# Chunk 0's state output as seven block products behind the last input projection, with two more rotations by transferred additions

## The chip, the cores and the metric

The kernel runs on one core of one Trainium2 chip. The metric is device time in microseconds (us), the median of several executions. Beside it stands one execution taken by the hardware profiler, with its span from the first to the last instruction and its trace. The engines are TensorE (PE, matmuls), VectorE (DVE), ScalarE (ACT), GpSimd (POOL, here mostly issuing DMAs that add) and SyncE (SP, issuing plain DMAs). A name such as L762 is a line of the kernel file.

## What is computed

The input `x` has 2048 rows of 512. It is normalised by row to `xn`, and three things are summed: `x` itself, a diagonal state-space layer on `xn`, and a gated feed-forward layer on `xn`.

```
xn   = layernorm(x)
Bu   = xn @ B_bar.T                      # complex, 512 states
h[t] = Lam_bar * h[t-1] + Bu[t]          # over all 2048 rows
y    = 2 * Re(h @ C.T) + xn * Dskip
ffn  = (silu(xn @ w_gate) * (xn @ w_up)) @ w_down     # 1376 hidden columns
out  = x + y + ffn
```

Matmuls take bf16 and sum in f32; the output is bf16.

## The kernel before

**Chunks.** The rows are cut into four chunks of 512 rows, and a chunk into four row tiles of 128. The transposed normalised input stands in `xnT`, one chunk after another. TensorE's order of stages, after a start-up for chunk 0, is: input projection (`bproj_chunk`, L974, 32 matmuls) and gate/up projection (`gateup_chunk`, L985, 84 matmuls) of chunks 0 and 1, projection of chunk 2, feed-forward output of chunk 0 (`out_ffn`, L743), two half tiles that chunks share (`up_halves`, L531), state output of chunk 0 (`out_ssm`, L753), gate/up of chunk 2, projection of chunk 3, feed-forward output of chunk 1, the rows of the last short hidden tile (`out_rows`, L591), state output of chunk 1 as seven products (`out_ssm_seven`, L644), gate/up of chunk 3, and the last pair of chunks (`out_pair`, L713).

**State layer.** A recurrence with complex factors is made real by a rotation: `u` is turned by a table of cosines and sines (`c16`, `s16`), scanned with a real decay (L459, eight scans per chunk), and turned back into `wt`. `rotation` (L384) does a turn with six VectorE instructions. `rotation_dma` (L413) does it with four and leaves two additions to GpSimd's DMAs, which add while they write; it needs a negated sine table `neg_s16`, which stands in the first chunk's columns of `xnT` once these have been used. Before, chunk 2's back rotation and chunk 3's forward rotation go this way.

**State output.** `out_ssm` multiplies `wt` (real and imaginary parts, 4 row blocks each) by `CF`, 32 matmuls of 512 columns for a chunk. `out_ssm_seven` does the same block matrix product with seven products of half size instead of eight (56 matmuls of 256 columns), with sums of blocks made beforehand: of the states by `state_sums` (L628), of the weights by `weight_sums` (L612). A sum is a copy by ScalarE, negated or not (`signed_copy`, L603), and a DMA that adds (`added`, L609). Afterwards VectorE puts the products together in f32 scratch that lies in a used gate/up buffer. Chunks 1 and 2 go this way before. Chunk 0's output sums stay in four of the eight PSUM banks from `out_ffn` until `out_rows` has added its part; then ScalarE copies them out (`out_leave`, L774) and a DMA adds them to the output, which already holds `x`.

**Order.** The order on each engine is that of the program text. VectorE's share of the state layer, of the normalisation and of the coefficients (`c_ops`, L354) is kept in a list, `backlog`, each item with a planned cost. `pump(us)` (L800) is called after each group of matmuls with its planned time and emits items while the time owed covers half the next one's cost; `need(tag)` emits all that is left up to the last item of a tag. `products` holds the gate times up multiplications, emitted by `multiply`. `spend` (L964) emits items of the list `sums`, the copies and additions of the block sums, some after each tile.

**Buffers that matter here.** All eight PSUM banks come from one pool. `gu_last` has two buffers, for even and odd chunks; L553 writes one and L527 (in `product_last`) reads it. `up_halves` emits L527 of chunks 0 and 1.

Of the kernel before, what the change touches and what calls it, by code (L numbers as in the profile page):

```python
# [10 lines left out]
F32 = mybir.dt.float32  # L11
BF16 = mybir.dt.bfloat16
ALU = mybir.AluOpType
# [10 lines left out]
def kernel(  # L24
# [52 lines left out]
    def flat(ap3):  # L77
        return ap3.rearrange("p q j -> p (q j)")
# [327 lines left out]

    neg_s16 = xnT[:, :, 0:CW]

    def negate_table():
        for q in range(NQ):  # L410
            nc.scalar.activation(out=neg_s16[:, q], in_=s16[:, q], func=ACT.Copy, scale=-1.0)

    def rotation_dma(src, dst, back):  # L413

        box = {}
        sines = (s16[:], neg_s16) if back else (neg_s16, s16[:])

        def side(i):
            t = box[i] = ssm.tile([128, NQ, CW], BF16, name="pm", bufs=3)
            V.tensor_tensor(out=t[:], in0=src()[:, i], in1=sines[i], op=ALU.mult)  # L420

        def main(i):
            V.tensor_tensor(out=dst()[:, i], in0=src()[:, i], in1=c16[:], op=ALU.mult)

        def join(i):
            nc.gpsimd.dma_start(out=dst()[:, i], in_=box[1 - i][:], accum_op=ALU.add)
# [59 lines left out]
    u_pair = {}  # L486
    products = []

# [6 lines left out]
    def gu_tile(c):  # L495
        if c not in gu_tiles:
            gu_tiles[c] = gut.tile([128, FT - 1, CW], BF16, name="guT")
        return gu_tiles[c]

    def u_tile(c, fi):  # L500
        if (c, fi // 2) not in u_pair:
            u_pair[c, fi // 2] = up_p.tile([128, 2, CW], BF16, name="u2")
        return u_pair[c, fi // 2]

    def product(c, fi):
        g, u = gu_tile(c)[:, fi - 1:fi + 1, :], u_tile(c, fi)[:]
        products.append(lambda: V.tensor_tensor(out=g, in0=g, in1=u, op=ALU.mult))  # L507
# [91 lines left out]
    TQ = [CT[:, i // 2, :, (i % 2) * HD:(i % 2 + 1) * HD] for i in range(4)]  # L599
    neg_b22 = BT[:, 1, :, 0:HD]  # L600
    parts = {NT - 1: part_end, NT - 2: jidx}

    def signed_copy(out, in_, sign):  # L603

        for lo in range(0, NQ, 2):
            yield lambda lo=lo: nc.scalar.activation(out=out[:, lo:lo + 2], in_=in_[:, lo:lo + 2], func=ACT.Copy,  # L606
                                                     scale=sign)

    def added(out, in_):  # L609
        yield lambda: nc.gpsimd.dma_start(out=out, in_=in_, accum_op=ALU.add)  # L610

    def weight_sums():  # L612

        (b11, b12), (b21, b22) = BQ
        t1, t2, t3, t4 = TQ
        for out, in_, sign, to, add in ((t3, b12, -1.0, t3, b22), (t1, b11, -1.0, t1, b12), (t2, b11, 1.0, t2, t3),
                                        (t4, b22, -1.0, t4, t1)):
            yield from signed_copy(out, in_, sign)
            yield from added(to, add)
        yield from added(t4, b21)  # L620

# [4 lines left out]
    s_tiles = {}  # L626

    def state_sums(c):  # L628

        (a11, a12), (a21, a22) = state_quarters(c)  # L630
        if c == 1:
            s1, s2, s3 = (ssm.tile([128, NQ, HW], BF16, name="cm", bufs=3) for _ in range(3))
            s4 = jidx[:].bitcast(BF16).rearrange("p (q j) -> p q j", q=NQ)
        else:
            s1, s2, s3, s4 = ((wg_g, wu_g)[i // 2][2][:, :, (i % 2) * HD:(i % 2 + 1) * HD] for i in range(4))
        s_tiles[c] = (s1, s2, s3, s4)
        for out, in_, sign, to, add in ((s1, a21, 1.0, s1, a22), (s3, a21, -1.0, s3, a11), (s2, a11, -1.0, s2, s1),
                                        (s4, a12, -1.0, s4, s2)):
            yield from signed_copy(out, in_, sign)
            yield from added(to, add)  # L640
        if c == 1:
            yield from signed_copy(neg_b22, BQ[1][1], -1.0)

    def out_ssm_seven(c):  # L644
# [4 lines left out]
        first = c * TPC  # L649
        space = flat(gu_tiles[c][:]).bitcast(F32).rearrange("p (s j) -> p s j", j=HD)  # L650
        high, low = (space[:, a:a + 4].rearrange("p (i h) j -> p i h j", h=2) for a in (2, 6))
        u2, five = high[:, :, 1], space[:, 0:2]

# [14 lines left out]
        def add(out, in0, in1):  # L668
            V.tensor_tensor(out=out, in0=in0, in1=in1, op=ALU.add)
            owed[0] -= 0.69  # L670
# [21 lines left out]
        x = taken(s1, t1)  # L692
        nc.scalar.copy(out=five, in_=x[:])
        if c == 1:
# [3 lines left out]
        seven = taken(s3, t3)  # L698
        add(low[:, :, 1], u2, five)
        skipped(0, low)  # L700
        product(a22, t4, at(1, 0), False, True)
        add(high[:, :, 0], seven[:], u2)
        add(high[:, :, 1], high[:, :, 0], five)
        skipped(1, high)
        product(s4, neg_b22, at(0, 1), False, True)
        if c == 1:
# [6 lines left out]
    def out_pair(c):  # L713

        multiply(0)
        for n in [*parts, *range(c * TPC, NT - len(parts))]:
            o_tiles[n] = [bank()]
        for op in state_sums(c):
            op()
# [10 lines left out]
        need(f"ssm{c}")  # L730
        need("skip")
        need(f"ssm{c + 1}")
        for n, part in parts.items():
# [229 lines left out]

    def spend(n, late=False):  # L964

        while n and sums:
            if sums[0] is None:
                if not late or any(item[3] == "ssm1" for item in backlog):
                    return
                sums[0:1] = state_sums(1)  # L970
            sums.pop(0)()
            n -= 1

    def bproj_chunk(c):  # L974
        need(f"ln{c}")
        for part in range(2):
            for q in range(NQ):
                bproj_tile(c, part, q)
                pump(BP)
                multiply(0 if q else 1)  # L980
                spend(1, c == NCH - 1)
                if c == NCH - 1 and part == 1 and q == 0:
                    load_rows()

    def gateup_chunk(c):  # L985
        for fi in [FT - 1, *range(FT - 1)]:
            gateup_tile(c, fi)
            pump(GU)
            multiply(1)
            spend(2)  # L990

    def out_chunk(c):

        multiply(0)
        for n in range(c * TPC, (c + 1) * TPC):
            out_ffn(n)
            pump(FT * 0.2163)
            if c == 1:
                spend(4, True)
# [5 lines left out]
        if c == 1:  # L1005
            for step in range(3):
                for k in range(2):
                    out_rows(k, step)
            for n in range(TPC):
                out_leave(n, o_tiles[n][0], opool.tile([128, D], BF16, name="res"))  # L1010
        need(f"ssm{c}")
        need("cf")
        if c == 1:
            spend(99, True)
            return out_ssm_seven(c)
        for n in range(c * TPC, (c + 1) * TPC):
            out_ssm(n)
            pump(2 * NQ * 0.2163)

# [16 lines left out]
    for part in range(2):  # L1036
        for q in range(NQ):
# [10 lines left out]
           ["ln2"] * len(norm2) + ["ln3"] * (len(stats3) + len(norm3)))  # L1048
    queue("cf", c_ops())
    load_late()  # L1050
# [7 lines left out]

    bproj_chunk(1)
    fwd1, back1, _ = ssm_ops(1)  # L1060
    queue("ssm1", fwd1 + back1)
    gateup_chunk(1)
# [4 lines left out]
    out_chunk(0)  # L1067
    sums += [*weight_sums(), None]
# [41 lines left out]
```

## Time and profile before

| what | value |
|---|---|
| median of 3 runs | 176.64 us (176.63 to 177.19) |
| the profiled execution, its own time | 177.04 us |
| its span | 175.2 us |
| granted TensorE clock, mean | 1.000 |
| DMA traffic | 21.36 MB, mean 122 GB/s |

A busy share is the time in which an engine had an instruction under way, as a share of the span. In a timeline each line gives the start, the length, the engine, the line of the kernel and the tile names (out<-in); a bracket tells how long the engine was idle before and what ended that. The chain lists, in order of time, the work that led without a gap to the last instruction. In the rows by stretch of time each engine has its busy time and, in brackets, its number of instructions; the last three columns are the granted clock, the busy share of the 16 DMA engines and what they moved in GB/s. A share a little above 1 comes from how packets are booked.

### The profile page before, as it was taken

To read this page: it belongs to the slowest core of one execution; us is meant where nothing else is said; L and a number is where in the kernel's file an instruction comes from. 1 tells how busy PE (TensorE), PEld (TensorE's weight loads), DVE (VectorE), ACT (ScalarE), POOL (GpSimd) and SP (SyncE) were. 2 spreads that over 40 slices of the span, in tenths; PEclk is the share of its full clock that TensorE was granted. 3 is DMA by queue.
4 is the path that set the end of the run, shared out by engine and by line. 5 is a ranking of instruction groups with operands and counts; after the bars stand their busy time and mean duration, and the time that the engine had idled before them with its cause. 6 is when DMAs were issued, how large, how long until landed. Compare 5 with 4: busy or idle time off the path is not lost.

```text
span 175.2 us, 2790 instructions
## 1 busy us (share of the span) xinstructions
PE 171.7 (98%) x1002; PEld 88.4 (50%) x1002; DVE 161.1 (92%) x248; ACT 107.6 (61%) x204; POOL 45.9 (26%) x49
## 2 busy tenths in 40 slices
PE   8999999999999999999999999999999999999993
PEld 2977544444444444444444444468444444447743
DVE  4779998999999997999999999999999999995884
ACT  5487898868598669772998699052486691001100
POOL 6050120000400130000352224136544841211440
PEclk9999999999999999999999999999999999999999
DMA  6998496995332013700399449339898999955034
GB/s 170 294 170 226 91 250 117 362 230 121 77 76 30 0 30 75 254 4 11 43 105 120 60 51 194 61 60 136 139 156 153 157 175 192 122 60 60 0 105 139
DMA packets 38974, 21.36 MB, mean 122 GB/s; under 512 B 22016, under 2 KB 38144, under 8 KB 38944
## 3 DMA queue, kind: packets, MB, share of 16 engines
q0 software_dynamic: 9552, 8.26, 34.0%
q1 hardware_dynamic: 28016, 12.30, 31.1%
q10 hardware_dynamic: 1392, 0.62, 1.3%
q8 instruction: 8, 0.13, 0.3%
q14 instruction: 6, 0.05, 0.1%
HBM read 8.33 MB, written 4.19 MB: 71 GB/s over the span
## 4 chain that ended last, share of the span: by engine, by line
PE 98%; DVE 0%; issue 0%
PE ps L492 35%; PE ps L380 16%; PE ps L724 10%; PE ps L750 10%; PE ps L762 8%; PE ps L657 7%; PE ps L851 2%; PE ps L828 2%; PE ps L550 2%; PE ps L932 2%; PE ps L595 2%; PE ps L539 1%; PE ps L245 1%; DVE res L767 0%; PE ps L275 0%
## 5 line engine op out<-in xcount | busy, mean ns | idle before, releaser
L492 PE MATMUL ps<-xnT,wg 128*128 128x512 bf16 (+1 forms) x148 | 36.6, 373 | 0.0
L492 PE MATMUL ps<-xnT,wu 128*128 128x512 bf16 (+1 forms) x148 | 36.6, 373 | 0.0
L459 DVE TENSOR_TENSOR_SCAN g<-r_t,car,u 128x512 bf16<-128x512 f32 x24 | 28.7, 1264 | 0.0
L380 PE MATMUL ps<-xnT,BT 128*128 128x512 bf16 x128 | 28.3, 379 | 0.0
L511 ACT ACTIVATE guT<-ps 128x512 bf16<-128x512 f32 (+1 forms) x40 | 24.0, 599 | 5.4 <-PE ps L492 3.4
L512 ACT CAST u<-ps 128x512 bf16<-128x512 f32 (+1 forms) x40 | 23.3, 583 | 4.7 <-PE ps L492 4.5
L492 PEld LDWEIGHTS <-wu 128*128 128x128 bf16 x148 | 14.5, 98 | 16.6
L492 PEld LDWEIGHTS <-wg 128*128 128x128 bf16 x148 | 14.4, 98 | 16.5
L382 ACT CAST u<-ps 128x512 bf16<-128x512 f32 x32 | 18.2, 586 | 4.0 <-PE ps L380 3.9
L380 PEld LDWEIGHTS <-BT 128*128 128x128 bf16 x128 | 12.5, 98 | 14.9
L750 PE MATMUL ps<-wd_sb,guT 128*128 128x512 bf16 x80 | 17.6, 379 | 0.0
L724 PE MATMUL ps<-wd_sb,guT 128*128 128x512 bf16 x80 | 17.4, 379 | 0.0
L214 POOL TENSOR_TENSOR rstd<-ve,neg_half 128x2 f32<-128x2 f32 (+1 forms) x4 | 5.7, 1415 | 44.9 <-DVE ve L213 44.9
L762 PE MATMUL ps<-CF,wt 128*128 128x512 bf16 (+2 forms) x80 | 14.2, 336 | 0.0
L507 DVE TENSOR_TENSOR guT<-guT,u 128x1024 bf16<-128x1024 bf16 x20 | 13.4, 679 | 0.0
L724 PEld LDWEIGHTS <-guT 128*128 128x128 bf16 x80 | 7.8, 98 | 9.4
L750 PEld LDWEIGHTS <-guT 128*128 128x128 bf16 x80 | 7.8, 98 | 9.4
L205 DVE BATCH_NORM_STATS2 stats<-xall 128x6 f32<-128x512 bf16 x14 | 9.5, 679 | 2.0 <-DMA xall<-in_A_x_dram 2.0
L610 POOL DMA_DIRECT2D CT<-CF x3 | 3.9, 1300 | 27.1 <-ACT CT L606 23.6
L690 ACT COPY guT<-ps 128x512 f32<-128x512 f32 x2 | 1.2, 586 | 15.8 <-PE ps L657 15.8
L762 PEld LDWEIGHTS <-wt 128*128 128x128 bf16 x80 | 7.1, 98 | 6.9 <-issue 0.4
L459 DVE TENSOR_TENSOR_SCAN g<-r_t,u 128x512 bf16<-128x512 f32 x8 | 9.3, 1205 | 0.0
(168 smaller groups left out, 265.0 us busy)
## 6 DMA issues: line engine op xcount, KB each, us to landing
wd_sb<-in_B_w_down_dram SPq DMA_DIRECT2D x2, 640.0 KB, 8.7
xall<-in_A_x_dram SPq DMA_DIRECT2D x1, 1024.0 KB, 6.2
out_dram<-res POOLq DMA_DIRECT2D x8, 128.0 KB, 3.8
wt<-pm POOLq DMA_DIRECT2D x2, 512.0 KB, 5.4
u<-pm POOLq DMA_DIRECT2D x2, 512.0 KB, 6.2
out_dram<-xall POOLq DMA_DIRECT2D x2, 512.0 KB, 10.2
CT<-CF POOLq DMA_DIRECT2D x3, 256.0 KB, 4.3
gu_rows<-ul SPq DMA_DIRECT2D x36, 8.0 KB, 1.8
```

What stands on the lines that cost most here:

```text
L205: nc.vector.bn_stats(out=stats[:, n, :], in_=xall[:, n, :])
L380: nc.tensor.matmul(ps[:], lhsT=BT[:, part, k, q * 128:(q + 1) * 128], rhs=xnT[:, k, c * CW:(c + 1) * CW], start=(k == 0), stop=(k == KD - 1))
L382: nc.scalar.copy(out=u_tiles[c][:, part, q, :], in_=ps[:])
L459: V.tensor_tensor_scan(out=g()[:, part, q, :], data0=r_t[:, q:q + 1].to_broadcast([128, CW]), data1=u_tiles[c][:, part, q, :], initial=ini ...
L492: nc.tensor.matmul(ps[:fs, lo:hi], lhsT=wslice(groups, fi, k), rhs=xnT[:, k, c * CW + lo:c * CW + hi], start=(k == 0), stop=(k == KD - 1))
L507: products.append(lambda: V.tensor_tensor(out=g, in0=g, in1=u, op=ALU.mult))
L511: nc.scalar.activation(out=gu_tile(c)[:, fi, 0:hi], in_=psg[:, 0:hi], func=ACT.Silu)
L512: nc.scalar.copy(out=u_tile(c, fi)[:, fi % 2, 0:hi], in_=psu[:, 0:hi])
L657: nc.tensor.matmul(place(i), lhsT=a[:, q, i * 128:(i + 1) * 128], rhs=b[:, q, :], start=(start and q == 0), stop=(stop and q == NQ - 1))
L724: nc.tensor.matmul(o[:], lhsT=gu_tiles[k][:, fi, i * 128:(i + 1) * 128], rhs=wd_sb[:, fi, :], start=(fi == 0), stop=False)
L750: nc.tensor.matmul(o[:], lhsT=gu_tiles[c][:, fi, i * 128:(i + 1) * 128], rhs=wd_sb[:, fi, lo:hi], start=(fi == 0), stop=False)
L762: nc.tensor.matmul(o, lhsT=w_tiles[c][:, part, q, i * 128:(i + 1) * 128], rhs=CF[:, part, q, lo:hi], start=(fresh and part == 0 and q == 0 ...
```

## The change

- Chunk 0's state output is done by `out_ssm_seven(0)` and no longer by `out_ssm`. It stands behind the projection of chunk 3 and ahead of chunk 1's feed-forward output. Its f32 scratch is the ring of up buffers, now one tile `u_all`, and used columns of `xnT`. Its last four adds (`leave_first`) stand behind `out_rows`, on VectorE, in place of the four copies by ScalarE.
- The block sums are written so that fewer copies are negated: those that keep their sign are plain DMAs from SyncE (`copied`), and the state sums of a chunk take four ScalarE copies in place of eight, the weight sums six in place of eight. The negated part of `CF` is no longer needed.
- Chunk 0's back rotation and chunk 1's forward rotation also go by `rotation_dma`. The negated sine table stands in `part_end` and `jidx`, two halves, and the instruction that reads it is split in two. It is made in the second gate/up stage.
- `skip_add` becomes a DMA that adds; the order of the skip items changes, and the stores of chunks 0 and 1 move to the end of `out_pair`'s skip.
- `need("ssm0")` and `need("cf")` come ahead of `up_halves`, and the coefficients (`cf`) stand between chunk 1's rotation and its scans.

```diff
-    neg_s16 = xnT[:, :, 0:CW]
+    neg_s16 = [t[:].bitcast(BF16).rearrange("p (q j) -> p q j", q=2) for t in (part_end, jidx)]
...
         def side(i):
             t = box[i] = ssm.tile([128, NQ, CW], BF16, name="pm", bufs=3)
-            V.tensor_tensor(out=t[:], in0=src()[:, i], in1=sines[i], op=ALU.mult)
+            if i == (1 if back else 0):
+                for h, table in enumerate(neg_s16):
+                    q = slice(2 * h, 2 * h + 2)
+                    V.tensor_tensor(out=t[:, q], in0=src()[:, i, q], in1=table, op=ALU.mult)
+            else:
+                V.tensor_tensor(out=t[:], in0=src()[:, i], in1=s16[:], op=ALU.mult)
...
-        ops = (rotation_dma if c == 3 else rotation)(lambda: u_tiles[c], lambda: u_tiles[c], False)
+        ops = (rotation_dma if c in (1, 3) else rotation)(lambda: u_tiles[c], lambda: u_tiles[c], False)
...
-        back = (rotation_dma if c == 2 else rotation)(g, wt, True)
+        back = (rotation_dma if c in (0, 2) else rotation)(g, wt, True)
...
     def skip_add():
-        V.tensor_tensor(out=xn_end[:], in0=xn_end[:], in1=xall[:, NT - TPC:NT, :], op=ALU.add)
+        nc.gpsimd.dma_start(out=xn_end[:], in_=xall[:, NT - TPC:NT, :], accum_op=ALU.add)
...
+    def copied(out, in_, pieces=1):
+        n = NQ // pieces
+        for lo in range(0, NQ, n):
+            yield 0, lambda lo=lo: nc.sync.dma_start(out=out[:, lo:lo + n], in_=in_[:, lo:lo + n])
...
+        s1, s2, s3, s4 = s_tiles[c] = [t[:] for t in state_places(c)]
+        yield from copied(s1, a21)
+        yield from copied(s4, a12)
+        yield from negated(s3, a21)
+        yield from added(s3, a11)
+        yield from added(s1, a22)
+        yield from negated(s2, a22)
+        yield from added(s2, s3)
+        yield from added(s4, s2)
...
         if c == 0:
             need("ln3")
+            need("ssm0")
+            need("cf")
             up_halves()
-            negate_table()
+            sums.extend(state_sums(0))
+            spend(0)
+            weights = list(weight_sums())
+            for _, op in weights[:2]:
+                op()
+            sums.extend(weights[2:])
             multiply(0)
+            spend(4)
+            return
+        for step in range(3):
+            for k in range(2):
+                out_rows(k, step)
+        leave_first()
         need(f"ssm{c}")
-        need("cf")
...
-        for n in range(c * TPC, (c + 1) * TPC):
-            out_ssm(n)
-            pump(2 * NQ * 0.2163)
+        out_ssm_seven(c)
...
     bproj_chunk(3)
+    load_rows()
+    need("ssm1")
+    sums += state_sums(1)
+    spend(99)
+    leave_first = out_ssm_seven(0)
     fwd3, back3, turns = ssm_ops(3)
     queue("ssm3", fwd3[:turns])
-    for c in range(NCH):
-        queue("skip", [(1.2, lambda c=c: skip_op(c)),
-                       (0.0, lambda c=c: skip_store(c)) if c < NCH - 1 else (1.2, skip_add)])
+    for c in (3, 2, 0, 1):
+        queue("skip", [(1.2, lambda c=c: skip_op(c))] + {3: [(0.0, skip_add)], 2: [(0.0, lambda: skip_store(2))]}.get(c, []))
     queue("ssm3", fwd3[turns:] + back3)
-    out_chunk(1)
+    out_chunk(1, leave_first)
```

More of the change, by code (lines that the diff above doesn't have):

```diff
@@ L486 @@
     u_pair = {}
+    u_all = const.tile([128, 4, 2, CW], BF16, name="u_all")
     products = []
@@ L615, in weight_sums @@
         t1, t2, t3, t4 = TQ
[L616 to L620, printed above, removed]
+        yield from sums_of(t1, t3, t2, t4, b11, b12, b22, b21)
     def state_quarters(c):
@@ L626, with halves, state_places @@
     s_tiles = {}
+    def halves(t, c):
+        return [t[:, :, c * CW + h * HW:c * CW + (h + 1) * HW] for h in range(2)]
+    def state_places(c):
+        if c == 0:
+            return halves(xnT, 0) + halves(xnT, 1)
+        if c == 1:
+            return [ssm.tile([128, NQ, HW], BF16, name="cm", bufs=3) for _ in range(3)] + halves(xnT, 2)[:1]
+        return halves(wg_g[2], 0) + halves(wu_g[2], 0)
     def state_sums(c):
         (a11, a12), (a21, a22) = state_quarters(c)
[L631 to L642, printed above, removed]
+        s1, s2, s3, s4 = s_tiles[c] = [t[:] for t in state_places(c)]
[7 more added lines that the diff above has]
+        yield from added(s4, s2)
     def out_ssm_seven(c):
@@ L692, in out_ssm_seven @@
         x = taken(s1, t1)
-        nc.scalar.copy(out=five, in_=x[:])
+        nc.scalar.copy(out=five, in_=split(x[:]))
         if c == 1:
@@ L698, in out_ssm_seven @@
         seven = taken(s3, t3)
-        add(low[:, :, 1], u2, five)
+        add(split(low[:, :, 1]), split(u2), five)
         skipped(0, low)
-        product(a22, t4, at(1, 0), False, True)
+        product(a22, t4, at(1, 0), False, c > 0)
         add(high[:, :, 0], seven[:], u2)
-        add(high[:, :, 1], high[:, :, 0], five)
+        add(split(high[:, :, 1]), split(high[:, :, 0]), five)
         skipped(1, high)
-        product(s4, neg_b22, at(0, 1), False, True)
+        product(s4, b22, at(0, 1), False, c > 0)
+        if c == 0:
+            return lambda: (finish(0, low), finish(1, high))
         if c == 1:
@@ L717, in out_pair @@
             o_tiles[n] = [bank()]
-        for op in state_sums(c):
+        for _, op in state_sums(c):
             op()
@@ L731, in out_pair @@
         need("skip")
+        skip_store(0)
+        skip_store(1)
         need(f"ssm{c + 1}")
@@ L962, with spend @@
     sums = []
[L964 to L972, printed above, removed]
+    def spend(n):
+        while sums and sums[0][0] <= n:
+            cost, op = sums.pop(0)
+            op()
+            n -= cost
     def bproj_chunk(c):
@@ L980, in bproj_chunk @@
                 multiply(0 if q else 1)
-                spend(1, c == NCH - 1)
-                if c == NCH - 1 and part == 1 and q == 0:
-                    load_rows()
+                spend(1)
     def gateup_chunk(c):
@@ L1048 @@
            ["ln2"] * len(norm2) + ["ln3"] * (len(stats3) + len(norm3)))
-    queue("cf", c_ops())
     load_late()
@@ L1059 @@
     bproj_chunk(1)
-    fwd1, back1, _ = ssm_ops(1)
-    queue("ssm1", fwd1 + back1)
+    fwd1, back1, turns = ssm_ops(1)
+    queue("ssm1", fwd1[:turns])
+    queue("cf", c_ops())
+    queue("ssm1", fwd1[turns:] + back1)
+    sums += negate_table()
     gateup_chunk(1)
```

57 lines of the change are left out of this document (31 added, 26 removed).

## The prediction

> **What bounds the kernel now.** I read the page first: the busy shares, the chain that ended last, and two groups of VectorE (DVE) whose prices I need.
>
> ```profile
> PE 171.7 (98%) x1002; PEld 88.4 (50%) x1002; DVE 161.1 (92%) x248; ACT 107.6 (61%) x204; POOL 45.9 (26%) x49
> ...
> PE 98%; DVE 0%; issue 0%
> ...
> L459 DVE TENSOR_TENSOR_SCAN g<-r_t,car,u 128x512 bf16<-128x512 f32 x24 | 28.7, 1264 | 0.0
> ...
> L507 DVE TENSOR_TENSOR guT<-guT,u 128x1024 bf16<-128x1024 bf16 x20 | 13.4, 679 | 0.0
> ```
>
> TensorE (PE) sets the end and never waits. But VectorE is busy 92% too, so I look next at how much room it has. The chain in order of time gives TensorE's stages:
>
> ```profile
> 72.24 1.85 PE ps L539 x16
> 74.09 7.01 PE ps L762 x32
> 81.10 0.86 PE ps L550 x4
> ...
> 114.77 1.41 PE ps L595 x24
> 116.17 6.22 PE ps L657 x56
> ...
> 157.79 1.41 PE ps L595 x24
> 159.20 6.36 PE ps L657 x56
> ```
>
> The reader sees chunk 0's state output (L762, 7.01) and the same work for chunk 1 as seven products (L657, 6.22). VectorE's timeline from there to the last pair:
>
> ```profile
> 117.81 0.13 DVE L468 TENSOR_TENSOR ct<-g,cos 128x4 f32<-128x4 bf16 x1
> ...
> 120.62 0.68 DVE L669 TENSOR_TENSOR guT<-ps,guT 128x512 f32<-128x512 f32 x1
> ...
> 123.53 2.48 DVE L669 TENSOR_TENSOR res<-ps,guT 128x512 bf16<-128x512 f32 x4
> ...
> 157.58 1.23 DVE L404 TENSOR_TENSOR wt<-pm 128x2048 bf16<-128x2048 bf16 x1
> 159.25 0.69 DVE L734 TENSOR_TENSOR part_end<-ps,xn_end 128x512 f32<-128x512 f32 x1 [0.45 <-PE ps L595]
> ```
>
> Between 120.62 and 158.8 it never waits, and it reaches the part adds (L734) 0.45 before TensorE lets it go on. All eight PSUM banks hold output sums there. The second product of the last pair (at 159.20 + 0.87 = 160.07) takes the bank that L734 frees at 159.94. So **two engines bound the end**: each microsecond that VectorE comes later than about half a microsecond stops TensorE.
>
> **The change, part by part.** *TensorE.* 32 matmuls of 512 columns (7.01) become 56 of 256 (6.22): **0.79 less**. The 7 us in which TensorE did L762 also gave other engines time after the half tiles (L539); now the next chunk's gate/up follows at 74.09.
>
> *The front: banks and ScalarE (ACT).* Chunk 0's four sums stay open in four banks, as before. The other four hold the short last tile (L550), the first tile's gate and up and the second tile's gate. The fifth group, at 74.09 + 4 x 0.86 = 77.55, needs the bank of L550, which L553 and L554 free.
>
> ```profile
> 73.27 2.38 ACT L543 CAST ul<-ps 64x512 bf16<-64x512 f32 x4 [0.99 <-PE ps L539]
> 75.55 2.19 ACT L411 ACTIVATE xnT<-s 128x512 bf16<-128x512 bf16 x4
> 82.00 0.59 ACT L553 ACTIVATE gu_last<-ps 96x512 bf16<-96x512 f32 x1 [4.26 <-PE ps L550]
> 82.61 0.58 ACT L554 CAST ul<-ps 32x512 bf16<-32x512 f32 x1
> ```
>
> Before, four negated copies of the sine table (2.19) stood behind L543, and ScalarE then sat idle for 4.26. That cover is gone. The sine copies move ahead into the second gate/up stage, but chunk 0's first two state sums put four copies of the same size in this place, ahead of L553. So L553 starts at 75.65 + 2.19 = 77.84, L554 ends near 79.05, and TensorE stands for 1.5. One more copy follows each tile and costs about 0.2 on the next bank: **1.7**.
>
> *The front: VectorE.* L553 overwrites `gu_last[0]`, so it also waits for the product of chunk 0's short tile (L527). I followed the planner's queue with its costs. The same rule gives for the kernel before exactly the order of VectorE that its timeline shows. For the new code the order is: rest of chunk 0's back rotation, four instructions of chunk 1's rotation, eight of L366, two scans, then L527.
>
> ```profile
> 62.88 1.22 DVE L400 TENSOR_TENSOR wt<-pm 128x2048 bf16<-128x2048 bf16 x1
> ...
> 69.24 4.07 DVE L366 SCALAR_TENSOR_TENSOR CF<-CT,nc2im,cm 128x512 bf16<-128x512 bf16 x6 [0.56 <-ACT cm L363]
> ```
>
> At 62.88 the new kernel does its last back instruction instead. Chunk 1's rotation then ends at 64.1 + 4.7 = 68.8 (four at about 1.15 and 0.1 for the split one, by L507: two halves at 0.68 for one at 1.22). Its transferred additions are issued near 67.6 and 68.8. The eight of L366 (4.07 / 6 = 0.68 each) end at 74.2, one scan (28.7 / 24 = 1.2) at 75.4. The second scan reads what the second addition writes. What such a pair takes:
>
> ```profile
> 132.43 0.85 POOL L426 DMA_DIRECT2D u<-pm  x1 [3.01 <-DVE pm L420]
> 133.69 0.85 POOL L426 DMA_DIRECT2D u<-pm  x1 [0.41 <-DVE u L423]
> ```
>
> ```profile
> DMA to landing us min/median/max: 4.7/5.4/7.8
> ```
>
> The first took 4.7 and the second 7.8, which is 4.4 after the first. That gives 67.6 + 4.7 + 4.4 = 76.7. But the copy of `A_x` to the output (L1065) is issued near 70 and fills the DMA engines:
>
> ```profile
> 70.00:72.00 2.00, 2.00 (x11) 0.80 (x9) 2.00 (x4) 2.00 (x4) 0.00 (x0) 1.00 1.07 341
> 72.00:74.00 2.00, 2.00 (x18) 0.82 (x16) 2.00 (x3) 0.98 (x3) 0.00 (x0) 1.00 0.58 229
> ```
>
> (1.07 + 0.58) x 2 = 3.3 of all engines. The second addition lands between 76.7 and 80.0; I take the middle, 78.4, as the two share the engines. Then a scan and L527 (1.6) end at 80.0, 2.1 later than ScalarE would be ready. Bounds: 0.4 and 3.7. **Front stall: 1.7 + 2.1 = 3.8**, between 2.1 and 5.4.
>
> *The tail.* Chunk 0's four finish adds stand right behind the out-rows matmuls (L595) on VectorE, and need them. When the out-rows of before ended, the copy L775 started:
>
> ```profile
> 115.98 2.05 ACT L775 CAST res<-ps 128x512 bf16<-128x512 f32 x4 [6.48 <-PE ps L595]
> ```
>
> So in the new kernel the finish adds start at 115.98 - 0.79 = 115.2, plus the front stall. VectorE is there earlier: the first adds of the new product stage wait for ScalarE's copy near 102.5 (four negated copies of chunk 1 stand ahead of it), take 2.9, and the planner, which no longer counts L762's 6.9 and takes off four adds, puts only one rotation instruction and five scans (7.1) behind them: 112.4. It idles 2.8. From the finish adds on it has the 38.2 of before (120.62 to 158.8), four finish adds (2.48), three more scans (3.6), the carry and two back instructions (117.81 to 120.62, 2.8), 0.2 for two split instructions, less the skip add that goes to a DMA (1.2): 46.1. The part adds start at 161.3 and free the bank at 162.0 instead of 159.94: **the end is 2.05 later**, the 0.79 already taken off. Two rotations save 2 x 2.3 on VectorE and the adds cost 5.3, so its busy sum hardly changes; what it loses is idle time that it can't make up.
>
> Chunk 3's second transferred addition is issued at 138.5 and by the 7.8 above lands at 146.3; its scan could start at 145.4: **0.9 more**, between 0 and 2.0. The upper end also covers the transferred skip add, which the part adds read and which now stands on GpSimd (POOL) behind the last pair's sums. Of before:
>
> ```profile
> 157.21 1.26 POOL L610 DMA_DIRECT2D wu<-wg  x1 [3.53 <-DMA wg<-wg]
> ```
>
> With three transfers of the skip taken out of their way, I expect those sums some four microseconds earlier, and the skip add near 161.
>
> *Edits costed at nothing.* Fewer negated copies in the sums: ScalarE is idle 39%. The new chunk's sums (four additions of the state, four of the weights) have from 78 to about 104. If that cover were gone, each 4.3 of lateness would stop TensorE as long. The two late stores have fifteen microseconds before the end; if they didn't, the last stores would wait.
>
> **Sum:** -0.8 + 3.8 + 2.85 + 0.9 = +6.75 on the profiled execution's 177.04: 183.8. That execution lies 0.4 above the median of the three runs, 176.64, so the forecast is 176.64 + 6.75 = **183.4** (180.8 to 186.1 by the bounds).
>
> **A rule to weigh.** The copy of `A_x` is one transfer of few, large packets (DMA view, 70.6 to 73.0):
>
> ```profile
> q1 hardware_dynamic: 18, 1.05, 119.9%
> ```
>
> 18 packets for 1.05 MB are 58 KB each, about one an engine. The Trainium skill ("DMA: Bandwidth & Descriptors", Queues, rings and completion order) says that an engine goes round its queues packet by packet and drains a whole one before it switches. By that rule the copy would go first; no row of before shows the two together.
>
> **Rivals.**
> - *Copy first* (18%): the addition waits for all of the copy, 80.0, front stall 5.4: 185.0. For it: the packet sizes. Against: the copy may be issued before or after the addition's packets are all under way.
> - *Clock lost* (14%): TensorE stands about 3.6 in front and 3.7 at the tail. At the start of the kernel ten matmuls, eight of 512 columns and two of 128, took
>
> ```profile
> 0.78 3.78 PE L828 MATMUL ps<-const-bfloat16-1.0 128*128 128x512 bf16 x10 [0.78 <-PEq L1094]
> ```
>
>  which is 0.44 per 512 columns (3.78 / 8.5) against 0.22 in L762 (7.01 / 32): 1.9 lost in that stretch. Once or twice on top: 185.3 to 187.2. Against it: no pause in before to see it by. The Trainium skill ("TensorE: Matmul & The Clock Gate", Part 1) puts the idle window at about 3.4 us, which these pauses would barely fill.
> - *One stall only* (14%): the tail alone gives 176.64 + 2.05 to 2.95, the front alone 176.64 - 0.79 + 3.8: 178.7 to 179.7.
> - *TensorE's saving comes through* (9%): 176.64 - 0.79 = 175.85. Its place is VectorE's queue ahead of chunk 0's finish adds: three scans more there (3.6) fill the idle 2.8, and the part adds are on time; with fewer it fails. It also needs a bank free at 77.55. For it: VectorE's busy sum is no larger than before. Against: the planner's order, and eight banks counted.
> - *Nothing to see* (4%): a stall as small as the saving, within 0.3%.
>
> The forecast keeps 41%. The range 178.7 to 187.0 leaves out the last two cases and part of the clock's: about 20%. A change of 0.3% is about what this measurement can tell from none. Faster 0.09, same 0.04, slower 0.87.
>
> **What would show it.** Front: TensorE with a wait of 2 to 5.5 in the first gate/up tiles behind L539, its releaser ScalarE, and L553 behind L527. VectorE idle before the second scan of chunk 1, released by a DMA, and 2.8 before chunk 0's finish adds, released by L595. Tail: TensorE idle 2.8 to 4.8 before the last pair's second product. I am wrong if TensorE has no wait at 77.5, or if VectorE has work until the finish adds can start.

## The result, and the profile after

| | before | after |
|---|---|---|
| median, us | 176.73 (176.59 to 177.30, 6 runs) | 211.19 (209.56 to 212.31, 6 runs) |
| ratio, 95% interval | 1 | 1.193 (1.187 to 1.199) |
| the profiled execution, its own time | 177.04 | 209.56 |
| its span | 175.2 | 207.8 |
| mean granted clock | 1.000 | 0.942 |

34.5 us slower, where 6.75 were forecast. Times and ratios here and below leave out disturbed executions, over 1.5% above the fastest of the same kernel (three of e10, one each of e4 and e5, two of e11, whose rows come from one of these).

The page of after: busy shares, TensorE (PE) and its granted clock in 40 slices, the chain's shares, and the two VectorE (DVE) groups. The chain reaches back only to 106.89, where the profile shows no cause, so its shares cover about half of the span.

```profile
PE 175.4 (84%) x1012; PEld 92.8 (45%) x1026; DVE 160.6 (77%) x255; ACT 102.8 (49%) x194; POOL 54.7 (26%) x57
...
PE   8999999999999947999970006999999999981994
...
PEclk9999999999999999999997555799999999998899
...
PE 26%; issue 10%; DMA 9%; ACT 2%; DVE 0%; POOL 0%; ACTq 0%; POOLq 0%; DVEq 0%
...
L464 DVE TENSOR_TENSOR_SCAN g<-r_t,car,u 128x512 bf16<-128x512 f32 x24 | 29.2, 1265 | 3.8 <-DMA u<-pm 3.8
...
L513 DVE TENSOR_TENSOR guT<-guT,u_all 128x1024 bf16<-128x1024 bf16 x20 | 13.5, 679 | 0.1
```

VectorE is as busy as before (160.6 against 161.1). TensorE has gaps in three places, and the clock drops behind two of them. Its timeline has these rows with a wait (in brackets: how long, and what ended it):

```profile
76.45 1.02 PE L545 MATMUL ps<-xnT,wu_last 128*64 128x512 bf16 x7 [2.92 <-DMA xnT<-xn_end]
...
82.03 1.02 PE L498 MATMUL ps<-xnT,wu 128*128 128x512 bf16 x4 [1.00 <-ACT ul L560]
83.30 1.02 PE L498 MATMUL ps<-xnT,wg 128*128 128x512 bf16 x4 [0.25 <-ACT guT L517]
...
126.66 1.68 PE L690 MATMUL ps<-CT,xnT 128*128 128x256 bf16 x7 [18.88 <-ACT xnT L726]
...
191.20 1.86 PE L690 MATMUL ps<-CF,wt 128*128 128x256 bf16 x8 [4.91 <-DVE part_end L771]
```

2.92 + 1.25 + 18.88 + 4.91 = 28.0 of waits. TensorE is also busy 3.7 longer (175.4 against 171.7) though the change saves 0.8, so about 4.5 went to half clock (a granted clock of 0.50). 28.0 + 4.5 - 0.8 = 31.7 of the 32.6 by which the span grew; the rest is in many short waits.

**The 18.88.** It stands in chunk 0's seven products. TensorE waits for ScalarE's (ACT) copy L726, which brings a product from PSUM into the scratch `five`. The chain around it, in order of time:

```profile
106.89 0.48 ACT u_all L723
107.36 18.13 issue
...
126.02 0.59 ACT xnT L726
126.61 0.05 issue
126.66 5.09 PE ps L690 x23
```

"issue" is time for which the profile shows no cause. The view of line L726 says that ScalarE stood at a semaphore (min, median and max in ns):

```profile
L726 ACTq EVENT_SEMAPHORE  x6: 38/38/19331, 106.0 to 125.6; - x6
```

In the program as built, L726 waits for one matmul, for eight transposes and for four additions by GpSimd (POOL), all of which write `xnT`. `five` is the second half of chunk 2's columns of `xnT`. The last of the four additions, `xnT<-cm`, makes chunk **1**'s fourth state sum and writes the first half of those columns: other columns, work for a later stage. It comes late. GpSimd's timeline and SyncE's (SPq is its DMA queue):

```profile
115.04 1.28 POOL L620 DMA_DIRECT2D cm<-wt  x1 [7.62 <-DMA cm<-wt]
115.79 1.44 POOL L620 DMA_DIRECT2D cm<-cm  x1
121.26 1.29 POOL L620 DMA_DIRECT2D xnT<-cm  x1 [4.03 <-issue]
```

```profile
79.87 29.65 SPq L188 DMA_DIRECT2D gu_rows<-ul  x36
109.62 2.04 SPq L182 DMA_DIRECT2D BT<-in_B_w_down_dram  x4
111.76 0.67 SPq L617 DMA_DIRECT2D cm<-wt  x1
112.53 0.65 SPq L617 DMA_DIRECT2D xnT<-wt  x1
```

Chunk 1's two plain copies (L617), new with the change, stand in SyncE's queue behind 36 row moves (L188, they gather the rows of the short hidden tile) that take 29.65 us to issue. Their sources are ready at 94.0 and 97.0, when VectorE ends the two parts of `wt`, but they go out only at 111.8; the additions on top of them follow to 121.3, and the last lands at about 125.5.

**Front and tail.** Rows of VectorE, then two of ScalarE:

```profile
78.24 1.28 DVE L464 TENSOR_TENSOR_SCAN g<-r_t,car,u 128x512 bf16<-128x512 f32 x1 [2.11 <-DMA u<-pm]
...
142.09 2.48 DVE L702 TENSOR_TENSOR res<-ps,u_all 128x512 bf16<-128x512 f32 x4 [5.27 <-PE ps L601]
...
190.45 0.69 DVE L771 TENSOR_TENSOR part_end<-ps,xn_end 128x512 f32<-128x512 f32 x1 [0.65 <-DMA xn_end<-xall]
```

```profile
78.58 2.19 ACT L611 ACTIVATE xnT<-wt 128x512 bf16<-128x512 bf16 x4
80.79 0.59 ACT L559 ACTIVATE gu_last<-ps 96x512 bf16<-96x512 f32 x1
```

The second scan waits for a landing at 78.2 (78.4 was forecast), and the four copies (2.19) stand ahead of L559 (L553 before), as forecast. The 2.92 at L545 was not in the forecast.

### The profile page after: what moved, and what is told of

It is laid out like the page before. It is cut to its first block, busy times and chain, and to the rows that moved or that the text cites. A ratio compares the mean times of both kernels' runs of the same rounds, so it can differ in the third digit from the quotient of the medians.

```text
span 207.8 us, 2870 instructions
## 1 busy us (share of the span) xinstructions
PE 175.4 (84%) x1012; PEld 92.8 (45%) x1026; DVE 160.6 (77%) x255; ACT 102.8 (49%) x194; POOL 54.7 (26%) x57
## 5 line engine op out<-in xcount | busy, mean ns | idle before, releaser
L498 PE MATMUL ps<-xnT,wu 128*128 128x512 bf16 (+1 forms) x144 | 35.9, 373 | 1.1 <-ACT ul L560 1.0
L464 DVE TENSOR_TENSOR_SCAN g<-r_t,car,u 128x512 bf16<-128x512 f32 x24 | 29.2, 1265 | 3.8 <-DMA u<-pm 3.8
L518 ACT CAST u_all<-ps 128x512 bf16<-128x512 f32 (+1 forms) x40 | 23.4, 585 | 4.4 <-PE ps L498 4.4
L498 PEld LDWEIGHTS <-wu 128*128 128x128 bf16 x148 | 14.5, 98 | 17.8 <-issue 1.3
L690 PE MATMUL ps<-CT,xnT 128*128 128x256 bf16 x24 | 3.7, 315 | 18.9 <-ACT xnT L726 18.9
L702 DVE TENSOR_TENSOR u_all<-u_all,xnT 128x512 f32<-128x512 f32 x2 | 1.4, 692 | 18.6 <-ACT xnT L726 18.6
L690 PEld LDWEIGHTS <-xnT 128*128 128x128 bf16 x40 | 4.5, 116 | 20.2 <-ACT xnT L726 19.2
L513 DVE TENSOR_TENSOR guT<-guT,u_all 128x1024 bf16<-128x1024 bf16 x20 | 13.5, 679 | 0.1
L719 POOL DMA_DIRECT2D out_dram<-res x8 | 7.1, 1268 | 24.6 <-DVE res L702 24.6
```

The lines of the kernel that those rows point to most:

```text
L464: V.tensor_tensor_scan(out=g()[:, part, q, :], data0=r_t[:, q:q + 1].to_broadcast([128, CW]), data1=u_tiles[c][:, part, q, :], initial=ini ...
L498: nc.tensor.matmul(ps[:fs, lo:hi], lhsT=wslice(groups, fi, k), rhs=xnT[:, k, c * CW + lo:c * CW + hi], start=(k == 0), stop=(k == KD - 1))
L518: nc.scalar.copy(out=u_tile(c, fi)[:, fi % 2, 0:hi], in_=psu[:, 0:hi])
L690: nc.tensor.matmul(place(i), lhsT=a[:, q, i * 128:(i + 1) * 128], rhs=b[:, q, :], start=(start and q == 0), stop=(stop and q == NQ - 1))
L719: nc.gpsimd.dma_start(out=out_v[:, n, :], in_=res[:], accum_op=ALU.add)
```

## The experiments

**e1: the scratch elsewhere.** `five` moves to a part of `BT` that is used up by then.

```diff
-            five = halves(xnT, 2)[1].bitcast(F32).rearrange("p (i a) j -> p i a j", i=2)
+            five = BT[:, 1, 0:2, :].bitcast(F32).rearrange("p i (a j) -> p i a j", a=2)
```

> The changed kernel, with chunk 0's scratch 'five' in the used half of BT (the imaginary input weights) and no longer in the columns of xnT. Theory A (ScalarE's copy L726 into 'five' waited for every earlier transfer into xnT, the last of them the addition into chunk 1's s4, because both stand in xnT): the wait of 18.9 us behind L726 is gone, and with it the slow stretch of TensorE after it (2.6): 211.2 - 21.5, about 187 to 190. What stays is some 4.9 in front and 5 to 6 at the tail. Rival B (the wait is for data that chunk 0's or chunk 1's products need anyway): TensorE waits as long at the same place or at chunk 1's products, 207 to 212.

190.33 us, ratio 1.074 (1.065 to 1.083): 20.9 less, a little above theory A's range, and no wait for L726 above 0.3. The wait was for a transfer into columns that L726 does not touch. Two rows of VectorE in e1 come back below:

```profile
81.47 1.28 DVE L464 TENSOR_TENSOR_SCAN g<-r_t,car,u 128x512 bf16<-128x512 f32 x1 [5.80 <-DMA u<-pm]
...
170.93 0.69 DVE L771 TENSOR_TENSOR part_end<-ps,xn_end 128x512 f32<-128x512 f32 x1 [0.68 <-DMA xn_end<-xall]
```

**e2: the late copies on another queue.** `five` stays in `xnT`; chunk 1's plain copies are issued by ScalarE.

```diff
-    def copied(out, in_, pieces=1):
+    def copied(out, in_, pieces=1, queue=nc.sync):
...
-            yield 0, lambda lo=lo: nc.sync.dma_start(out=out[:, lo:lo + n], in_=in_[:, lo:lo + n])
+            yield 0, lambda lo=lo: queue.dma_start(out=out[:, lo:lo + n], in_=in_[:, lo:lo + n])
...
-        yield from copied(s1, a21)
-        yield from copied(s4, a12)
+        yield from copied(s1, a21, queue=nc.scalar if c == 1 else nc.sync)
+        yield from copied(s4, a12, queue=nc.scalar if c == 1 else nc.sync)
```

> The changed kernel with 'five' left in xnT; only the two plain copies of chunk 1's state sums are issued by ScalarE's DMA queue and not by SyncE's, where they stood behind 36 row moves until 111.8. Theory A with its second half (how long L726 waits is set by SyncE's queue): s4's addition lands some 5 to 6 us earlier, near 120, and the whole is 204 to 207. Rival B (the chain of additions on GpSimd sets it, whatever SyncE does): no change, 209 to 212.

207.90 us, 3.3 less, between the two. The copies went out 3.5 us earlier (108.2 and 109.0; in ScalarE's order they stand behind the last copies of the projection, up to 108.1), but the additions on top of them still followed one after the other, and L726 still waited for the last:

```profile
125.71 1.68 PE L690 MATMUL ps<-CT,xnT 128*128 128x256 bf16 x7 [14.00 <-ACT xnT L726]
```

So the row moves make the wait longer; the dependency makes it.

**e3: the copy of `A_x` later** (on top of e1).

```diff
-    nc.sync.dma_start(out=out[0, 0:(NT - 2 * TPC) * 128, :], in_=A_x[0, 0:(NT - 2 * TPC) * 128, :])
...
     gateup_chunk(2)
+    nc.sync.dma_start(out=out[0, 0:(NT - 2 * TPC) * 128, :], in_=A_x[0, 0:(NT - 2 * TPC) * 128, :])
     bproj_chunk(3)
```

> As e1_five_own, and the copy of A_x to the output is issued behind gate/up of chunk 2, no longer ahead of chunk 0's feed-forward output. Theory C (TensorE's 2.9 us in up_halves are for chunk 3's transposes, held up by this copy and the transferred additions together; the same copy holds the addition for which VectorE waits 2.1): both waits shrink, 2 to 3.5 us less than e1. Rival D (the transposes are late because normalisation is late, 63.5 in place of 62.8, and the additions are in their way): less than 1 us.

189.31 us, 1.0 less, which is within the spread of the two (e1: 188.43 to 191.13). Half of theory C holds: the addition lands 4.3 earlier and TensorE has no wait for the bank. The other half fails: the wait for chunk 3's transposes stays (3.04 in e1), so this copy does not make it.

```profile
76.35 1.31 PE L545 MATMUL ps<-xnT,wu_last 128*64 128x512 bf16 x7 [3.12 <-DMA xnT<-xn_end]
```

```profile
77.17 1.29 DVE L464 TENSOR_TENSOR_SCAN g<-r_t,car,u 128x512 bf16<-128x512 f32 x1 [1.28 <-DMA u<-pm]
```

But almost none of it reaches the end. VectorE waits later instead, and its first part add of the last pair (L771, called the pair add below) starts at 170.82 against 170.93 in e1. The end of that story needs the table below.

**e4: three scans ahead of the finish adds** (on top of e1).

```diff
+        for _ in range(3):
+            emit()
         leave_first()
```

> As e1_five_own, and three more of the planner's items (scans) are emitted ahead of chunk 0's finish adds. Theory E (VectorE's idle time ahead of these adds, 2.8 us in the prediction, comes back at the tail as TensorE's wait for the part adds): the idle time fills, TensorE's wait at the tail falls by 2 to 3.5 and the slow stretch after it goes too: 3 to 5 us less than e1. Rival F (the tail waits for the transferred skip add behind the last sums on GpSimd): less than 1 us.

187.97 us, 2.4 less. The wait of 2.77 ahead of the finish adds is gone, but VectorE then waits 1.01 and 2.14 for ScalarE's next tiles at L513, and L771 starts only 0.5 sooner (170.44). The rest of the gain is clock: TensorE's pause at the pair is 2.68 instead of 4.97 and no half clock follows. The tail wait shrinks as E has it, but mostly because TensorE itself comes to the pair 1.8 later (its bank wait in front is 4.13 here, 2.42 in e1). That the idle time comes back at the tail is not borne out.

**e5: the cover given back** (on top of e1). Six groups of the third gate/up stage go ahead of the half tiles of chunks 2 and 3 and of the short tile.

```diff
-        for fi in [FT - 1, *range(FT - 1)]:
+        tiles = [FT - 1, *range(FT - 1)]
+        for fi in tiles if c != 2 else [0, 1, 2, FT - 1, *range(3, FT - 1)]:
+            if c == 2 and fi == FT - 1:
+                up_half(2)
```

> On top of e1_five_own (190.33 us): the half tiles of chunks 2 and 3 and the short last tile move three tiles (six groups, 5.2 us of TensorE) into the third gate/up stage; no work is added or left out. Theory G (lost cover: the block L762 that was moved away had hidden both the late transposes of chunk 3 and the wait for the bank of the short tile): both waits of TensorE in front (3.04 and 2.17 + 0.25) go, and with them the 1.6 at half clock behind the first; VectorE's waits for TensorE behind them (2.42 and 2.77) shrink by as much, so most of it reaches the end: 5 to 6.5 less, 184 to 185.5. Rival H (VectorE sets the end, and its wait of 5.80 for the second transferred addition is not touched): the front waits go, but the end gains less than 2.5.

187.24 us, 3.1 less. TensorE's waits in front fall from 5.5 to 1.0, and the half clock goes, as G says; the end gains little more than H allows. VectorE waits 5.07 ahead of the finish adds in exchange, and TensorE 2.14 and 2.10 for block sums.

**e6: chunk 0's back rotation in the plain form** (on top of e1).

```diff
-        back = (rotation_dma if c in (0, 2) else rotation)(g, wt, True)
+        back = (rotation_dma if c == 2 else rotation)(g, wt, True)
```

> On top of e1_five_own (190.33 us): chunk 0's back rotation by the plain form of six VectorE instructions; the other new transferred rotation (chunk 1 forward) stays. Theory I (the two additions of 512 KB of this rotation crowd the transposes of chunk 3 and hold up L214 in GpSimd's queue): the wait of the half tiles for the transposes (3.04) falls below 1 and the half-clock stretch behind it goes; VectorE has 2.3 more to do, and the net gain is 1 to 3. Rival J (it is the copy of A_x or chunk 1's own additions that delay the transposes): the wait stays above 2, and the time is 0 to 2.5 longer.

201.19 us, 10.9 **more**, so theory I's gain did not come. In front its mechanism holds: no wait at L545. The landing times of chunk 3's four transposes, for before, after and e6:

```profile
DMA to landing us min/median/max: 2.3/2.3/2.4
```

```profile
DMA to landing us min/median/max: 2.4/4.6/6.7
```

```profile
DMA to landing us min/median/max: 2.3/2.3/2.3
```

The loss is elsewhere. With two more instructions in the planner's list, the second addition of chunk 3's rotation is emitted behind the last block sums, and waits for them in GpSimd's queue:

```profile
158.68 1.27 POOL L620 DMA_DIRECT2D wu<-wg  x1 [3.55 <-DMA wg<-wu]
159.43 1.41 POOL L431 DMA_DIRECT2D u<-pm  x1
```

VectorE's scans of chunk 3 wait for it, and TensorE then waits 16.70 at the pair:

```profile
166.00 8.34 DVE L464 TENSOR_TENSOR_SCAN g<-r_t,car,u 128x512 bf16<-128x512 f32 x7 [11.92 <-DMA u<-pm]
```

**e7: scans by part** (on top of e1). Chunks 1 and 3 scan the four blocks of the part that lands first, then the other.

```diff
-        for q in range(NQ):
-            for part in range(2):
+        for i in range(2 * NQ):
+            for part, q in (divmod(i, NQ) if c in (1, 3) else divmod(i, 2)[::-1],):
```

> On top of e1_five_own (190.33 us): the eight scans of chunks 1 and 3 run first over the four blocks of the part whose addition lands first, then over the other part (same scans, other order). Theory K (the second scan's wait for the landing of the second addition is what makes L533, and so the bank of the short tile, late): VectorE's wait of 5.80 falls below 2.5, ScalarE's wait of 1.93 for L533 goes, TensorE's bank wait falls from 2.4 to the 1.25 that the four copies make, and the wait of 1.71 in chunk 3 goes too: 2 to 4 less. Rival L (nothing of it reaches the end, because TensorE waits for something else by as much): less than 1.

187.99 us, 2.3 less. VectorE's waits of 5.80 and 1.71 for landings are gone, and the bank wait falls to 0.36. K holds.

**e8 and e9: the edits together.** e8 is e5 + e7 + the three steps, `A_x` ahead of the second gate/up stage, chunk 1's sums queued ahead of `bproj_chunk(3)` and their plain copies on ScalarE's queue. e9 leaves those sums where they were, puts the copies on GpSimd's queue, and lets one negated copy, not four, stand ahead of the third gate/up stage.

```diff
-    bproj_chunk(3)
-    load_rows()
     need("ssm1")
     sums += state_sums(1)
+    bproj_chunk(3)
+    load_rows()
     spend(99)
```

> On top of e1_five_own: the edits of e5 and e7, the three planner steps of e4_steps, the copy of A_x ahead of the second gate/up stage, chunk 1's state sums queued ahead of the projection of chunk 3, and their two plain copies on ScalarE's DMA queue. If the waits are separate and add up (2.8 + 1.6 + 2.4 in front, 5.0 + 1.0 at the tail of e1), 178 to 180; if VectorE, as busy as before, still runs late into the last pair, 181 to 184. Less than the 176.7 of before needs VectorE without any wait from 64 to 158 us.

191.96 us: worse than e1, and above both forecasts. ScalarE itself stood still:

```profile
103.84 0.68 ACTq L616 DMA_DIRECT2D cm<-wt  x1
104.61 0.81 ACTq L616 DMA_DIRECT2D xnT<-wt  x1
105.47 0.63 ACT L610 ACTIVATE cm<-wt 128x512 bf16<-128x512 bf16 x1 [10.26 <-issue]
```

The source of chunk 1's block sums was ready at 94.7. In the program as built, the issue of each copy also waits for one of SyncE's row moves, because the two transfers count on the same completion semaphore. TensorE stood 8.58 for the projection tiles that ScalarE should have copied out in that time.

> As e8_combined, but chunk 1's state sums stand where the change has them, their two plain copies go on GpSimd's queue, and one negated copy instead of four stands ahead of the third gate/up stage. Theory M (the waits in front are separate, each taken away by its own edit, and VectorE then has no wait until the end of chunk 0's back rotation): TensorE waits less than 1 in front, 0 to 1 for chunk 1's sums, and 0.5 to 2.5 at the pair adds, because VectorE is as busy as before: 176.5 to 179. Rival N (a new queue takes over: the plain copies on GpSimd hold up the additions behind them): a wait above 2 at the products of chunk 0 or 1, 180 or more.

```diff
-        yield from copied(s1, a21)
-        yield from copied(s4, a12)
+        yield from copied(s1, a21, queue=nc.gpsimd if c == 1 else nc.sync)
+        yield from copied(s4, a12, queue=nc.gpsimd if c == 1 else nc.sync)
...
-            spend(4)
+            spend(1)
```

181.25 us, ratio 1.022 (1.018 to 1.026). The waits in front are gone and the one at the pair adds is in theory M's range, but the time is 2 above it; N has the time, and its wait at the products is 1.98 where it asks for more than 2. TensorE's two waits above 0.3:

```profile
106.05 1.03 PE L689 MATMUL ps<-CT,wt 128*128 128x256 bf16 x8 [1.98 <-DMA CT<-CT]
...
164.39 1.03 PE L689 MATMUL ps<-CF,wt 128*128 128x256 bf16 x8 [2.40 <-DVE part_end L770]
```

**e10: chunk 0's finish by ScalarE and DMAs** (on top of e9, without the steps). The last two additions of chunk 1's state sums also move, behind chunk 0's products.

```diff
+                    nc.gpsimd.dma_start(out=out_v[:, 2 * half + i, :], in_=extra[:, i].rearrange("p h j -> p (h j)"),
+                                        accum_op=ALU.add)
+            return lambda: [out_leave(n, o_tiles[n][0], opool.tile([128, D], BF16, name="res")) for n in range(TPC)]
-            return lambda: (finish(0, low), finish(1, high))
```

> As e9_combined_b without the three planner steps, and chunk 0's four finish adds leave VectorE: ScalarE copies the four sums out as before the change, and GpSimd's queue adds both those and the four f32 block sums to the output. Theory O (VectorE's busy time is what bounds the end): VectorE is 2.5 less busy, does not wait for the out rows any more, and is on time at the pair adds: TensorE's 0.8 comes through, 175.5 to 177. Rival P (eight more additions crowd GpSimd's queue and the DMA engines behind 108 us): chunk 1's sums or the next gate/up stage, which writes over the f32 sums, wait, and the time is 178 or more.

180.67 us (180.2 to 181.0), ratio 1.021 (1.019 to 1.024). VectorE is 2.7 less busy and the pair wait falls to 0.75, as O says, but the time is above O's range. TensorE's wait for block sums at chunk 0's products falls too (1.98 to 0.56); a new one for the rows of `BT` is 1.03. VectorE stands 5.95 for chunk 1's products instead. No version here beats the kernel before.

**e11 and e12: one part alone.** e11 is the change without chunk 0's seven products. e12 is e1 without the two rotations, and with three planner steps ahead of the last pair.

```diff
-    leave_first = out_ssm_seven(0)
+    def leave_first():
+        for n in range(TPC):
+            out_leave(n, o_tiles[n][0], opool.tile([128, D], BF16, name="res"))
...
-            spend(4)
+            for n in range(TPC):
+                out_ssm(n)
+                pump(2 * NQ * 0.2163)
             return
```

> The change without its first part: chunk 0's state output by 32 matmuls behind the half tiles and its sums leaving through ScalarE, as before; the two further transferred rotations, the fewer negated copies, the transferred skip add and the late stores stay. Theory Q (the transferred rotations alone make the half tiles wait for chunk 3's transposes): TensorE waits 2 to 3.2 at L545, with up to 1.6 more at half clock behind it; L762 hides the rest of the front, VectorE has 4.6 less to do, and the tail is on time: 179 to 182. Rival R (what costs in front is the lost cover of L762 alone, not the transfers): no wait at L545 above 0.5, 176 to 177.5.

184.3 and 186.2 us, ratio 1.048 (1.041 to 1.054): without the seven products the rest of the change costs some 8 us. Theory Q's wait is there: TensorE waits 4.48 for chunk 3's transposes, and half clock follows. But the rest is not the rotations alone. Later VectorE waits 5.38 for a result buffer that chunk 0's stores still read, and TensorE 2.39 behind it. These stores land after 10.6 us (3.8 before). GpSimd issues them right behind chunk 2's two additions of 512 KB, which stand behind chunk 1's block sums, and these are late because their plain copies left SyncE at 111.2, behind the row moves, as in after. No run parts the two causes.

```profile
77.48 1.89 PE L545 MATMUL ps<-xnT,wu_last 128*64 128x512 bf16 x7 [4.48 <-DMA xnT<-xn_end]
```

```diff
-        ops = (rotation_dma if c in (1, 3) else rotation)(lambda: u_tiles[c], lambda: u_tiles[c], False)
+        ops = (rotation_dma if c == 3 else rotation)(lambda: u_tiles[c], lambda: u_tiles[c], False)
...
-        back = (rotation_dma if c in (0, 2) else rotation)(g, wt, True)
+        back = (rotation_dma if c == 2 else rotation)(g, wt, True)
```

> On top of e1_five_own (190.33 us): both further rotations by the plain form, and three planner steps ahead of the last pair, which keep the additions of chunk 3's rotation ahead of the last block sums in GpSimd's queue. So the seven products of chunk 0 without the rotations that make room on VectorE. Theory S (VectorE sets the end: its busy time grows by 4.6, while only its wait of 5.8 and TensorE's 3.0 + 1.6 in front go): the waits of L545 and of the second scan vanish, the bank wait of 1.3 to 2.5 stays, and TensorE waits 4 to 8 at the pair adds: 182 to 187. Rival T (the transferred rotations cost more than they give): 181 or less.

195.45 us, 5.1 more than e1: theory S in kind, larger in size. L545 does not wait; the banks cost 4.1 in front, and the pair waits longest.

```profile
175.63 1.86 PE L690 MATMUL ps<-CF,wt 128*128 128x256 bf16 x8 [10.05 <-DVE part_end L773]
```

**What holds them together.** For nine kernels, the waits in the brackets of VectorE's timeline from 62 us to the first pair add (L734 before, L771 after) are added up and taken from the start of that add. This is bookkeeping: what is left over is 62 us and VectorE's busy time from there on.

| kernel | pair add starts | VectorE's waits | difference |
|---|---|---|---|
| before | 159.25 | 1.9 | 157.4 |
| after | 190.45 | 33.5 | 157.0 |
| e1 | 170.93 | 14.5 | 156.4 |
| e3 | 170.82 | 14.1 | 156.8 |
| e5 | 169.49 | 13.0 | 156.5 |
| e7 | 168.72 | 12.1 | 156.7 |
| e9 | 163.66 | 6.7 | 156.9 |
| e10 | 162.56 | 8.6 | 154.0 |
| e12 | 174.89 | 13.3 | 161.6 |

The other kernels give 157.0 (e2), 156.7 (e4), 156.5 (e8), 159.0 (e6, with two more instructions) and 151.4 (e11, without chunk 0's product adds). So the difference moves only where work was added (e6, e12) or taken away (e10, e11). The end comes 15.9 to 18.4 us behind the pair add in the table (longer where half clock follows). In before and e11 the pair add itself waits for TensorE (0.45 and 5.53); in the others VectorE comes last, in after, e1 and e2 with up to 0.7 of waiting for the skip add. So what counts of the change is that it took VectorE's waits from 1.9 to 33.5. A wait that an edit took away counted only where it did not come back further on: in e3 the sum fell only from 14.5 to 14.1, and in e5 to 13.0. What e5 gained beyond that is clock: the end comes 15.9 behind its pair add, and 17.6 in e1.

## Why the prediction was wrong

- **The failed step** is "Edits costed at nothing": "The new chunk's sums ... have from 78 to about 104". That is chunk 0's. The edit also turned chunk 1's two copies into SyncE transfers, and I did not follow SyncE's queue, in which they stand behind 36 row moves; nor did I ask what else waits for a transfer into `xnT`, in which the change put both a sum and the scratch. In place of nothing it was 18.88 and the half clock behind it (20.9 in the medians, by e1). The step's own sentence gave the right price: lateness there stops TensorE as long.
- **Front, 3.8 forecast.** The bank stall by the four copies was 1.25 for 1.7: right in kind. The second addition's 2.1 was 0 in after, where it landed at 78.2; in e1, e2 and e4 it landed near 81.5 and made the bank stall 2.4 to 4.2. What I left out is the wait for chunk 3's transposes, 2.92: the additions of chunk 0's rotation crowd them (e6). The front came to 4.17 by other parts than mine: that the size is near is luck.
- **Tail, 3.75 forecast, 4.91 measured.** VectorE's idle time ahead of the finish adds, forecast as 2.8, was 2.77 in e1 (5.27 in after, behind the long stall). The second addition of chunk 3 (0.9 forecast) was 1.67, and the skip add, put in the upper bound, came 0.65 late. The waits are the ones named, and longer. That the idle time ahead of the finish adds makes the tail late is not shown: in e4 it was filled, and the pair add started only 0.5 sooner.
- **TensorE's saving** was there: chunk 0's group of 56 took 6.11 at full clock (e7). It never reached the end, because VectorE came late to the pair: the reading of "two engines bound the end" is what the table bears out.
- **Rivals.** "Clock lost" (1.9 a pause) took place on top, about 4.5 for two pauses. "Copy first" did not happen: the two transfers shared the engines. In e1 the copy took 10.8 where it took 5.4 before, and the second addition 11.7, so both ended near 81.5:

```profile
out_dram<-in_A_x_dram SPq DMA_DIRECT2D x1, 10.8
```

```profile
DMA to landing us min/median/max: 5.5/8.6/11.7
```

## What to carry to other kernels

When a second engine is busy nine tenths of the time, add up its waits, before and after: here their sum said how late the end was, and a saving on the other engine did not show. Take a wait away only after asking where on that engine it will come back. When an edit turns an engine's copy into a transfer, read the whole queue it is put on, and list every instruction that waits for a transfer into the same buffer, other columns included. Scratch for one stage does not belong in a buffer into which another stage's transfers are still to land.

## What the runs showed of the hardware

- **Half clock after short pauses.** The granted clock is the last but two column (after, behind the 18.88):

```profile
126.00:128.00 2.00, 1.34 (x7) 0.97 (x8) 0.69 (x1) 0.58 (x1) 0.00 (x0) 0.50 0.05 12
...
134.00:136.00 2.00, 2.00 (x11) 0.92 (x10) 2.00 (x3) 0.00 (x0) 0.00 (x0) 1.00 0.00 0
```

  From 62 us on, every pause of TensorE of 3.0 us or more in these runs was followed by a clock of 0.50, for about 3 to 6 us. Of the shorter ones some were (1.96 in e3, 2.10 in e5, 2.68 in e7) and some were not (2.92 in after, 2.83 in e7, 2.68 in e4). The Trainium skill ("TensorE: Matmul & The Clock Gate", Part 1) gives an idle window of about 3.4 us; here pauses well below it were sometimes enough, and the measurement decides.
- **Transposes are held up by additions.** Chunk 3's four transposes landed after 2.3 us where chunk 0's rotation left no addition beside them (before, e6), and after up to 6.8 us beside its additions of 512 KB (e1, and e3, where the copy of `A_x` came later).
- **Queues wait for each other.** A DMA issued by ScalarE went out at 103.84, though its data were ready at 94.7 (e8): in the program as built it shares a completion semaphore with one of SyncE's row moves and waits for that move.
